# Load order, row statistics on two engines, and the last output tile of a fused attention and gMLP kernel

## The chip, the cores and the metric

The kernel runs on one core of one Trainium2 chip. Time is that of the device, in microseconds (us), for one execution; several runs are made and their median is given. A profile is one execution of its own, recorded by the hardware profiler. Engine names in it: PE is TensorE (PEld its weight loads), DVE is VectorE, ACT is ScalarE, POOL is GpSimd, SP is SyncE, which here issues DMAs.

## What is computed

Two blocks share one normalised input, and their outputs are added to the input (S = 2048 tokens, D = 512):

```python
xn = _layernorm(x)                       # no gain, no bias, eps 1e-5
# A: sliding, dilated attention, 32 heads of 16, 8 keys per token at distance 0, 2, .. 14
qkv = xn @ wqkv
logits = (q . k[shifted]) * 16 ** -0.5   # masked where the key lies before the start
a = softmax(logits) . v[shifted]  @ wo
# B: gMLP with a spatial gate
z = gelu(xn @ w_in)                      # 2048 x 1376
z1, z2 = z[:, :688], layernorm(z[:, 688:])
b = (z1 * (w_sp @ z2 + b_sp)) @ w_out    # w_sp is 2048 x 2048
out = x + a + b
```

All inputs and the output are bfloat16.

## The kernel before

Tokens are cut into 16 tiles of 128. The order of work is written out by hand: each engine runs its instructions in program order, and semaphores for the true dependencies are set by the framework.

**Loads.** All loads are issued by SP, in the order of lines 165 to 180: x tile 0 (128 KB), x tiles 1 to 3, `w_z2` (the half of `w_in` that gives z2) in two column halves of 344, then `wqk` in four parts between x blocks 1 and 2 (four tiles each), `wv`, the gate's bias, and x block 3. The x blocks use three buffers, so block 3 waits for block 0.

**Normalising the input.** For each token tile VectorE computes mean and variance (`ln_stats`, L187 and L188). Tiles 0 to 3 get their inverse root from ScalarE's Sqrt (`roots`, L196) and a reciprocal on VectorE; tiles 4 to 15 get it from two Newton steps of three operations each, behind three seed operations on integers, all on VectorE (`ln_newton`, L202 to L208), for four tiles at a time. `ln_apply` (L192) writes the normalised tile. It is transposed into `xnT` by TensorE for tiles 0 to 3 (`transpose_pe`, L213, with a copy on ScalarE for tiles 0 and 1, L215, and on VectorE for tiles 2 and 3, L217), and by a DMA issued by SP for the others (`transpose_dma`, L220).

**The opening.** `spin` issues matmuls on ones that nobody reads. Tile 0 is normalised, transposed and multiplied by `w_z2` (`z2_start`, L226, 8 matmuls of 344 columns: two column halves by four chunks of the contraction); then tile 1; then tiles 2 and 3 are normalised and transposed. All statistics of tiles 4 to 15 stand next in VectorE's order. TensorE goes on with `qk_chunk` (L258: for 512 tokens and 128 channels of q and of k, 8 matmuls of 512 columns), with z2 tiles 2 and 3 between the chunks, then z2 tiles 4 to 6 and the chunks of the next 512 tokens, and so on. ScalarE empties each result: Gelu for z2 (L232), a square for its statistics (L236), copies for q and k (L261). Three pairs of PSUM banks go round (`bank_pair`).

**The middle.** VectorE multiplies q by shifted k (`products`, L287), TensorE sums them over each head's channels (`reduce_heads`, L296), and softmax follows; v comes from `v_pair` (L271). For each output tile j the spatial mix (`mix`, L463, 32 matmuls) and z1 (`z1_tile`, L475) give the gated product, which a DMA transposes into `uT` (L486). VectorE meanwhile forms the attention output `op` (`av_ops`, L529 to L538), in portions that `vector_work` hands out.

**The end.** `op` holds 14 of each head's 16 channels for direct use; the other two are copied by `op_rest` (L518, eight DMAs for each half of the tokens) into free rows of the last chunk of `uT`. The output tiles are formed in two passes (`pair`, L587) over two groups of four tiles: 112 matmuls of `op` by `wo_r` (L597), then for each tile six of `uT` by `wout` (L605). VectorE adds x (L609) and SP writes the tile out (L610).

Of the kernel before, what the change touches and what calls it, by code (L numbers as in the profile page):

```python
# [45 lines left out]
def kernel(  # L46
# [38 lines left out]
    def bank_pair(name, two=False):  # L85
        turn[0] += 1
        pool = ps_b if turn[0] % 3 == 0 and not two else ps_a
        return pool.tile([P, 2, 512], F32, name=name, tag="mm")
# [71 lines left out]
    def load_x(b):  # L160
        t = xqp.tile([P, 4, D], BF16, name="xq")
        SP.dma_start(t[:], x2[b * 4 * P:(b + 1) * 4 * P, :].rearrange("(i p) d -> p i d", p=P))
        xq.append(t)

    x0 = xqp.tile([P, 4, D], BF16, name="xq")
    SP.dma_start(x0[:, 0, :], x2[0:P, :])
    SP.dma_start(x0[:, 1:4, :], x2[P:4 * P, :].rearrange("(i p) d -> p i d", p=P))  # L167
    xq.append(x0)
    for hh in range(2):
        fsl = slice(hh * FHALF, (hh + 1) * FHALF)  # L170
        SP.dma_start(w_z2[:, :, fsl], w_in_r[:, :, FH + hh * FHALF:FH + (hh + 1) * FHALF])  # L171
    wqk_s = wqkv_r[:, :, 0:2 * D].rearrange("p k (s n) -> p k s n", s=2)
    for ch in range(2):
        csl = slice(ch * D // 2, (ch + 1) * D // 2)
        for s in range(2):
            SP.dma_start(wqk[:, :, s, csl], wqk_s[:, :, s, csl])
        load_x(1 + ch)
    SP.dma_start(wv[:], wqkv_r[:, :, 2 * D:3 * D])
    SP.dma_start(b16[:], B_b_sp.rearrange("(j p) -> j p", p=P))
    load_x(3)  # L180
# [4 lines left out]
    def ln_stats(i):  # L185
        xs = xq[i // 4][:, i % 4, :]
        V.bn_stats(stats[:, i, :], xs)  # L187
        V.bn_aggr(mv[:, i, :], stats[:, i, :])  # L188
# [9 lines left out]
    def ln_newton(a, b):  # L198

        sl = slice(a, b)  # L200
        y, h, t = rstd[:, sl], hv[:, sl], nt[:, sl]
        V.tensor_scalar(h, mv[:, sl, 1], EPS, -0.5 / NEWTON_K, ALU.add, ALU.mult)  # L202
        V.tensor_scalar(t.bitcast(I32), h.bitcast(I32), 1, 0x3FFFFFFF, ALU.logical_shift_right, ALU.bitwise_and)
        V.tensor_scalar(y.bitcast(I32), t.bitcast(I32), -1, SEED, ALU.mult, ALU.add)
        for c in NEWTON_C:
            V.tensor_tensor(t, y, y, ALU.mult)
            V.tensor_tensor(t, t, h, ALU.mult)
            V.scalar_tensor_tensor(y, t, c, y, ALU.add, ALU.mult)  # L208

    def transpose_pe(i, xn):  # L210
        pt = ps_aux.tile([P, C, P], BF16, name="pt", tag="aux")
# [9 lines left out]

    def z2_start(i):
        pz = bank_pair("pzb")
        for hh in range(2):
            for kc in range(C):
                PE.matmul(pz[:, hh, 0:FHALF], xnT[:, kc, i * P:(i + 1) * P],  # L226
                          w_z2[:, kc, hh * FHALF:(hh + 1) * FHALF],
                          start=(kc == 0), stop=(kc == C - 1))
        return pz

    def z2_gelu(i, pz):
        A.activation(z2[:, i, :].rearrange("p (a b) -> p a b", a=2), pz[:, :, 0:FHALF],  # L232
# [5 lines left out]
    def z2_tile(i):  # L238
        z2_gelu(i, z2_start(i))
# [13 lines left out]
    def qk_chunk(b, c):  # L253
        tsl = slice(b * 512, (b + 1) * 512)
        pq = bank_pair("pq")
        for s in range(2):
            for kc in range(C):
                PE.matmul(pq[:, s, :], wqk[:, kc, s, c * P:(c + 1) * P], xnT[:, kc, tsl],  # L258
                          start=(kc == 0), stop=(kc == C - 1))
        at = HALO + b % 2 * 512  # L260
        A.copy(qk[b // 2][:, :, c, at:at + 512], pq[:])  # L261

    wv_v = wv[:].rearrange("p k (h d) -> p k d h", d=DH)
    xnT_g = xnT[:].rearrange("p c (b k t) -> p c b k t", b=NB, k=NG)
# [65 lines left out]
        wsps[j] = t  # L330


    ln_stats(0)
    roots(0, 1)
    V.reciprocal(rstd[:, 0:1], rstd[:, 0:1])
    transpose_pe(0, ln_apply(0))
    spin(4)
    pz0 = z2_start(0)
    ln_stats(1)
    roots(1, 2)  # L340
    ln_stats(2)
    V.reciprocal(rstd[:, 1:2], rstd[:, 1:2])
    transpose_pe(1, ln_apply(1))
    spin(4)
    pz1 = z2_start(1)
    ln_stats(3)
    roots(2, 4)
    z2_gelu(0, pz0)
    z2_gelu(1, pz1)
    V.reciprocal(rstd[:, 2:4], rstd[:, 2:4])  # L350
    xn2 = ln_apply(2)
    xn3 = ln_apply(3)
    transpose_pe(2, xn2)
    transpose_pe(3, xn3)
    spin(3)


    for b in range(4, NT, 4):
        for i in range(b, b + 4):
            ln_stats(i)  # L360
        ln_newton(b, b + 4)
        for i in range(b, b + 4):
            transpose_dma(i, ln_apply(i))


    qk_chunk(0, 0)
    qk_chunk(0, 1)
    z2_tile(2)
    z2_square(0)
    qk_chunk(0, 2)  # L370
    z2_tile(3)
    qk_chunk(0, 3)
    z2_square(1)
    pb = ps_aux.tile([P, NT], BF16, name="pb", tag="aux")
    PE.transpose(pb[:], b16[:], ident[0:NT, 0:NT])
    A.copy(b_col[:], pb[:])
# [134 lines left out]
    wout = late2.tile([P, MCH, D], BF16, name="wout")  # L511
    G.memset(wout[32:64, MCH - 1, :], 0.0)

    def op_rest(hb):

        for k in range(NG):
            for e in range(2):
                SP.dma_start(uT[64 + 32 * e:96 + 32 * e, MCH - 1, hb * SB + k * TG:hb * SB + (k + 1) * TG],  # L518
                             op[32 * k:32 * k + 32, DHA + e, hb * TG:(hb + 1) * TG])

    def av_ops():
        for hb in range(NB):
            for q in range(2):
                osl = slice(hb * TG + q * P, hb * TG + (q + 1) * P)
                pws = []
                for p in range(4):
                    off = HALO - DIL * (W - 1 - 2 * p) + q * P
                    pw = pwp.tile([P, 2, DH, P], BF16, name="pw")
                    V.tensor_tensor(pw[:], shifted(vp[:, :, hb, off:off + P]),  # L529
                                    a_sb[:, 2 * p:2 * p + 2, osl].unsqueeze(2).broadcast_to([P, 2, DH, P]), ALU.mult)  # L530
                    yield 2.3
                    pws.append(pw)
                    if p % 2 == 1:
                        V.tensor_tensor(pws[p - 1][:], pws[p - 1][:], pw[:], ALU.add)  # L534
                        yield 2.3
                V.tensor_tensor(pws[0][:], pws[0][:], pws[2][:], ALU.add)
                yield 2.3
                V.tensor_tensor(op[:, :, osl], pws[0][:, 0], pws[0][:, 1], ALU.add)  # L538
                yield 1.2
            if hb == 0:  # L540
                softmax_norm(1, smp)
                yield 5.5
# [19 lines left out]
    for j in range(3, NT):  # L562
        z1_tile(j, mix(j))
        if j == 3:
            pair_b.close()
            ps_o = [ctx.enter_context(tc.tile_pool(name="ps_o0", bufs=4, space=PSUM, reuse_waits="tile"))]
        vector_work(4.6)
        gate_out(j - 1)
        if j == 5:
            SP.dma_start(wout[:, 0:MCH - 1, :], B_w_out[0:(MCH - 1) * P, :].rearrange("(m p) n -> p m n", p=P))  # L570
            SP.dma_start(wout[0:FTAIL, MCH - 1, :], B_w_out[(MCH - 1) * P:FH, :])
            for e in range(2):
                SP.dma_start(wout[64 + 32 * e:96 + 32 * e, MCH - 1, :],
                             A_wo.rearrange("(h d) n -> d h n", d=DH)[DHA + e])
        if 6 <= j < 10:
            k = j - 6
            SP.dma_start(wo_r[32 * k:32 * k + 32, :, :], A_wo.rearrange("(h d) n -> h d n", d=DH)[:, 0:DHA, :])
        if 11 <= j < 13:
            load_xr(j - 11)
        if j == 13:  # L580
            op_rest(0)
    gate_out(NT - 1)
    pair_a.close()


    ps_o.append(ctx.enter_context(tc.tile_pool(name="ps_o1", bufs=4, space=PSUM, side="right", reuse_waits="tile")))
    for pair in range(2):  # L587
        if pair:
            vector_work(1e9)
            op_rest(1)  # L590
        pos = {}
        for jj in (2 * pair, 2 * pair + 1):
            for k in range(NG):
                pos[jj, k] = ps_o[jj % 2].tile([P, D], F32, name="po")
            for d in range(DHA):
                for k in range(NG):
                    PE.matmul(pos[jj, k][:], op[32 * k:32 * k + 32, d, jj * P:(jj + 1) * P],  # L597
                              wo_r[32 * k:32 * k + 32, d, :],
                              start=(d == 0), stop=False, tile_position=(32 * k, 0))
        for jj in (2 * pair, 2 * pair + 1):  # L600
            hb, q = jj // 2, jj % 2
            for k in range(NG):
                i = 8 * hb + 2 * k + q
                for m in range(MCH):
                    PE.matmul(pos[jj, k][:], uT[:, m, i * P:(i + 1) * P], wout[:, m, :],  # L605
                              start=False, stop=(m == MCH - 1))
                vector_work(2.0)
                ot = otp.tile([P, D], BF16, name="ot")
                V.tensor_tensor(ot[:], pos[jj, k][:], xrs[jj][:, k, :], ALU.add)  # L609
                SP.dma_start(out2[i * P:(i + 1) * P, :], ot[:])  # L610
            if jj + 2 < 4:
                load_xr(jj + 2)

# [29 lines left out]
```

## Time and profile before

| | |
|---|---|
| median of 3 runs | 210.63 us (210.3 to 211.45) |
| the profiled execution | 211.15 us |
| its span, first to last instruction | 208.8 us |
| PE busy, share of the span | 201.8 us, 97% |
| DVE busy | 166.8 us, 80% |
| ACT busy | 93.1 us, 45% |
| POOL busy | 6.0 us, 3% |
| granted TensorE clock | 1.0 of full speed |

The page cuts the span into 40 slices of 5.2 us. TensorE's row reads 7 in the first slice and 3 in the last, and 9 (90% or more busy) in nearly all between. VectorE is at 4 to 9 in the first nine slices. GpSimd does its few operations in the first 4 us (masks and a unit matrix) and clears small pads later.

Two costs stand beside the matmuls of the opening: the 16 statistics of L187 take 670 ns each, and the 16 applications of L192 take 409 ns each. The median load of `w_z2` lands 5.0 us after its issue, that of an x block 6.6 us after, an output tile 1.7 us after.

### The profile page before, as it was taken

The page shows a single profiled execution, that of the slowest core. Times are in us where ns is not written, and L with a number is a line of the kernel's source. Part 1 is how long each engine was busy: PE and PEld are TensorE (multiplying, and loading weights), DVE is VectorE, ACT ScalarE, POOL GpSimd, SP SyncE. Part 2 cuts the span into 40 slices and gives each one's busy share as a digit, 9 for nine tenths or more (in the row PEclk, how much of TensorE's full clock was granted, in tenths as well). Part 3 has the DMA queues.
Part 4 walks back from the last instruction along what each step waited for, and adds up shares of the span by engine and source line. Part 5 has one row for each costly group of instructions (what it writes and reads, how often), then busy time and mean ns, then how long its engine had stood idle before and what let it go on. Part 6 is the DMA issues. An engine that isn't in the chain of part 4 may idle for free.

```text
span 208.8 us, 3966 instructions
## 1 busy us (share of the span) xinstructions
PE 201.8 (97%) x1638; PEld 118.0 (57%) x1645; DVE 166.8 (80%) x198; ACT 93.1 (45%) x144; POOL 6.0 (3%) x34
## 2 busy tenths in 40 slices
PE   7799999999999999999999999999999999999993
PEld 4445544454556665556666666666666664444441
DVE  4689986986187699999999999999999965582252
ACT  3468888766788998326733121233333221000000
POOL 5000000000000000000000000000000000000000
PEclk9999999999999999999999999999999999999999
DMA  6993335999000003442965999999654232038332
GB/s 168 312 331 82 76 75 102 171 262 205 5 0 3 3 0 22 104 100 52 150 149 128 228 163 223 199 189 193 145 148 108 56 72 48 25 78 255 92 107 78
DMA packets 68817, 25.62 MB, mean 123 GB/s; under 512 B 57168, under 2 KB 68672, under 8 KB 68672
## 3 DMA queue, kind: packets, MB, share of 16 engines
q1 hardware_dynamic: 68800, 25.38, 56.6%
q8 instruction: 13, 0.21, 0.4%
q14 instruction: 4, 0.03, 0.0%
HBM read 9.79 MB, written 2.10 MB: 57 GB/s over the span
## 4 chain that ended last, share of the span: by engine, by line
PE 94%; DMA 3%; DVE 1%; SPq 1%; issue 1%; ACT 0%
PE pg L463 36%; PE pq L258 13%; PE po L605 10%; PE pz L475 9%; PE pzb L226 9%; PE pv L271 7%; PE po L597 6%; PE pl L296 4%; DMA w_z<-in_B_w_in_dram 3%; DVE xnT L217 0%; DVE ot L609 0%; ACT xnT L215 0%; SPq L171 0%; PE pt L213 0%; SPq L167 0%
## 5 line engine op out<-in xcount | busy, mean ns | idle before, releaser
L463 PE MATMUL pg<-z,wspT 128*128 128x344 bf16 x512 | 77.3, 309 | 0.0
L463 PEld LDWEIGHTS <-wspT 128*128 128x128 bf16 x512 | 49.9, 98 | 25.2 <-issue 0.8
L287 DVE TENSOR_TENSOR pr<-qk 128x8192 bf16<-128x8192 bf16 x8 | 35.1, 4421 | 6.5 <-PE pl L296 6.5
L466 ACT ACTIVATE gs<-pg,b_col 128x688 bf16<-128x688 f32 x16 | 13.4, 835 | 54.0 <-PE pg L463 54.0
L529 DVE TENSOR_TENSOR pw<-vp,a_sb 128x4096 bf16<-128x4096 bf16 x16 | 36.1, 2283 | 0.0
L258 PE MATMUL pq<-xnT,wqk 128*128 128x512 bf16 x123 | 28.9, 379 | 0.7 <-DVE xnT L217 0.4
L609 DVE TENSOR_TENSOR ot<-po,xr 128x512 bf16<-128x512 f32 x16 | 10.9, 688 | 16.4 <-PE po L605 16.3
L226 PE MATMUL pzb<-w_z,xnT 128*128 128x344 bf16 x128 | 20.7, 309 | 1.5 <-DMA w_z<-in_B_w_in_dram 1.0
L475 PE MATMUL pz<-w_z,xnT 128*128 128x344 bf16 x128 | 21.3, 309 | 0.0
L605 PE MATMUL po<-wout,uT 128*128 128x512 bf16 x94 | 20.6, 379 | 0.3 <-issue 0.3
L258 PEld LDWEIGHTS <-wqk 128*128 128x128 bf16 x128 | 12.3, 98 | 15.0 <-issue 1.4
L261 ACT CAST qk<-pq 128x1024 bf16<-128x1024 f32 x16 | 16.2, 1012 | 8.4 <-PE pq L258 8.2
L534 DVE TENSOR_TENSOR pw<-pw 128x4096 bf16<-128x4096 bf16 x8 | 18.3, 2287 | 0.1
L226 PEld LDWEIGHTS <-xnT 128*128 128x128 bf16 x128 | 12.1, 98 | 9.5 <-issue 2.0
L475 PEld LDWEIGHTS <-xnT 128*128 128x128 bf16 x128 | 12.4, 98 | 6.8 <-issue 0.8
L605 PEld LDWEIGHTS <-uT 128*128 128x128 bf16 x96 | 9.2, 98 | 11.7 <-issue 0.8
L271 PE MATMUL pv<-xnT,wv 128*32 128x512 bf16 x256 | 14.9, 380 | 0.0
L480 ACT ACTIVATE z<-pz 128x688 bf16<-128x688 f32 x16 | 11.9, 744 | 5.6 <-PE pz L475 4.8
L236 ACT ACTIVATE junk<-z 128x688 bf16<-128x688 bf16 x16 | 12.5, 780 | 0.1
L597 PE MATMUL po<-wo_r,op 32*128 32x512 bf16 x224 | 12.4, 374 | 0.0
L232 ACT ACTIVATE z<-pzb 128x688 bf16<-128x688 f32 x16 | 11.8, 740 | 0.6 <-PE pzb L226 0.6
L187 DVE BATCH_NORM_STATS2 stats<-xq 128x6 f32<-128x512 bf16 x16 | 10.7, 670 | 1.7 <-DMA xq<-in_A_x_dram 1.7
(73 smaller groups left out, 139.2 us busy)
## 6 DMA issues: line engine op xcount, KB each, us to landing
xr<-in_A_x_dram SPq DMA_DIRECT2D x4, 512.0 KB, 4.8
out_dram<-ot SPq DMA_DIRECT2D x16, 128.0 KB, 1.7
wo_r<-in_A_wo_dram SPq DMA_DIRECT2D x4, 448.0 KB, 4.9
xq<-in_A_x_dram SPq DMA_DIRECT2D x3, 512.0 KB, 6.6
wqk<-in_A_wqkv_dram SPq DMA_DIRECT2D x4, 256.0 KB, 6.2
w_z<-in_B_w_in_dram SPq DMA_DIRECT2D x2, 344.0 KB, 5.0
w_z<-in_B_w_in_dram SPq DMA_DIRECT2D x1, 688.0 KB, 6.6
wout<-in_B_w_out_dram SPq DMA_DIRECT2D x1, 640.0 KB, 5.0
```

What stands on the lines that cost most here:

```text
L226: PE.matmul(pz[:, hh, 0:FHALF], xnT[:, kc, i * P:(i + 1) * P], w_z2[:, kc, hh * FHALF:(hh + 1) * FHALF], start=(kc == 0), stop=(kc == C - 1))
L258: PE.matmul(pq[:, s, :], wqk[:, kc, s, c * P:(c + 1) * P], xnT[:, kc, tsl], start=(kc == 0), stop=(kc == C - 1))
L261: A.copy(qk[b // 2][:, :, c, at:at + 512], pq[:])
L271: PE.matmul(pv[32 * k:32 * k + 32, dd, :].rearrange("p (b t) -> p b t", b=NB), wv_v[:, kc, 2 * d2 + dd, :], xnT_g[:, kc, :, k, :], start=( ...
L287: V.tensor_tensor(pr[:], qk[hb][:, 0, :, HALO:HALO + SB].unsqueeze(1).broadcast_to([P, 2, C, SB]), shifted(qk[hb][:, 1, :, off:off + SB]), ...
L463: PE.matmul(pg[:, hh, 0:FHALF], wsps[j][:, k, :], z2[:, k, hh * FHALF:(hh + 1) * FHALF], start=(k == 0), stop=(k == NT - 1))
L466: A.activation(gs[:], pg[:, :, 0:FHALF], ACT.Identity, bias=b_col[:, j:j + 1])
L475: PE.matmul(pz[:, hh, 0:FHALF], xnT[:, kc, j * P:(j + 1) * P], w_z1[:, kc, hh * FHALF:(hh + 1) * FHALF], start=(kc == 0), stop=(kc == C - 1))
L529: V.tensor_tensor(pw[:], shifted(vp[:, :, hb, off:off + P]), a_sb[:, 2 * p:2 * p + 2, osl].unsqueeze(2).broadcast_to([P, 2, DH, P]), ALU.mult)
L534: V.tensor_tensor(pws[p - 1][:], pws[p - 1][:], pw[:], ALU.add)
L597: PE.matmul(pos[jj, k][:], op[32 * k:32 * k + 32, d, jj * P:(jj + 1) * P], wo_r[32 * k:32 * k + 32, d, :], start=(d == 0), stop=False, til ...
L605: PE.matmul(pos[jj, k][:], uT[:, m, i * P:(i + 1) * P], wout[:, m, :], start=False, stop=(m == MCH - 1))
```

## The change

There are three edits.

1. *The opening.* The loads are issued in another order: x tiles 0 and 1 singly, the first two contraction chunks of `w_z2` (full rows of 688 columns), x tiles 2 and 3, the other two chunks, x block 1, `wqk` in two parts (q, then k), x block 2, and so on. Tiles 0 to 3 are normalised with one root each. z2 tiles 0 and 1 run their first two chunks ahead of the other two, and z2 tiles 2 and 3 run ahead of any q or k. A chunk of q and k becomes `qk_pair` for the first 512 tokens: two chunks of q, or of k, in one bank pair. There are fewer `spin` matmuls.
2. *The roots of tiles 4 to 15* are formed for two tiles at a time. The seeds stay on VectorE; each Newton step is four operations on GpSimd, and a pair's tiles are normalised after the statistics and seeds of the next pair.
3. *The end.* The second `op_rest` moves ahead of the second group's matmuls of the first pass and is issued by ScalarE's queue. The last output tile is formed in two column halves of 256, in new PSUM banks; its attention part and x are added ahead of time into `rest`.

```diff
     SP.dma_start(x0[:, 0, :], x2[0:P, :])
-    SP.dma_start(x0[:, 1:4, :], x2[P:4 * P, :].rearrange("(i p) d -> p i d", p=P))
+    SP.dma_start(x0[:, 1, :], x2[P:2 * P, :])
+    SP.dma_start(w_z2[:, 0:2, :], w_in_r[:, 0:2, FH:F])
+    SP.dma_start(x0[:, 2:4, :], x2[2 * P:4 * P, :].rearrange("(i p) d -> p i d", p=P))
+    SP.dma_start(w_z2[:, 2:4, :], w_in_r[:, 2:4, FH:F])
     xq.append(x0)
-    for hh in range(2):
-        fsl = slice(hh * FHALF, (hh + 1) * FHALF)
-        SP.dma_start(w_z2[:, :, fsl], w_in_r[:, :, FH + hh * FHALF:FH + (hh + 1) * FHALF])
-    wqk_s = wqkv_r[:, :, 0:2 * D].rearrange("p k (s n) -> p k s n", s=2)
-    for ch in range(2):
-        csl = slice(ch * D // 2, (ch + 1) * D // 2)
-        for s in range(2):
-            SP.dma_start(wqk[:, :, s, csl], wqk_s[:, :, s, csl])
-        load_x(1 + ch)
+    load_x(1)
+    for s in range(2):
+        SP.dma_start(wqk[:, :, s, :], wqkv_r[:, :, s * D:(s + 1) * D])
+    load_x(2)
...
         for c in NEWTON_C:
-            V.tensor_tensor(t, y, y, ALU.mult)
-            V.tensor_tensor(t, t, h, ALU.mult)
-            V.scalar_tensor_tensor(y, t, c, y, ALU.add, ALU.mult)
+            G.tensor_tensor(t, y, y, ALU.mult)
+            G.tensor_tensor(t, t, h, ALU.mult)
+            G.tensor_scalar(t, t, c, None, ALU.add)
+            G.tensor_tensor(y, y, t, ALU.mult)
...
+    def z2_part(i, pz, kc):
         for hh in range(2):
-            for kc in range(C):
-                PE.matmul(pz[:, hh, 0:FHALF], xnT[:, kc, i * P:(i + 1) * P],
+            PE.matmul(pz[:, hh, 0:FHALF], xnT[:, kc, i * P:(i + 1) * P],
...
+    def qk_pair(b, s, c2):
+        tsl = slice(b * 512, (b + 1) * 512)
+        pq = bank_pair("pq")
+        for cc in range(2):
+            c = 2 * c2 + cc
+            for kc in range(C):
+                PE.matmul(pq[:, cc, :], wqk[:, kc, s, c * P:(c + 1) * P], xnT[:, kc, tsl],
+                          start=(kc == 0), stop=(kc == C - 1))
+        at = HALO + b % 2 * 512
+        A.copy(qk[b // 2][:, s, 2 * c2:2 * c2 + 2, at:at + 512], pq[:])
...
+    def recip(i):
+        V.reciprocal(rstd[:, i:i + 1], rstd[:, i:i + 1])
     ln_stats(0)
     roots(0, 1)
-    V.reciprocal(rstd[:, 0:1], rstd[:, 0:1])
-    transpose_pe(0, ln_apply(0))
-    spin(4)
-    pz0 = z2_start(0)
     ln_stats(1)
     roots(1, 2)
+    recip(0)
+    transpose_pe(0, ln_apply(0))
+    recip(1)
+    spin(2)
+    transpose_pe(1, ln_apply(1))
+    spin(2)
+    pz0 = bank_pair("pzb")
+    pz1 = bank_pair("pzb")
+    for i, pz in ((0, pz0), (1, pz1)):
+        for kc in range(2):
+            z2_part(i, pz, kc)
     ln_stats(2)
...
+    roots(2, 3)
     ln_stats(3)
-    roots(2, 4)
+    roots(3, 4)
+    for kc in range(2, C):
+        z2_part(0, pz0, kc)
     z2_gelu(0, pz0)
-    z2_gelu(1, pz1)
-    V.reciprocal(rstd[:, 2:4], rstd[:, 2:4])
+    recip(2)
     xn2 = ln_apply(2)
+    recip(3)
     xn3 = ln_apply(3)
     transpose_pe(2, xn2)
+    for kc in range(2, C):
+        z2_part(1, pz1, kc)
     transpose_pe(3, xn3)
-    spin(3)
-    for b in range(4, NT, 4):
-        for i in range(b, b + 4):
-            ln_stats(i)
-        ln_newton(b, b + 4)
-        for i in range(b, b + 4):
-            transpose_dma(i, ln_apply(i))
-    qk_chunk(0, 0)
-    qk_chunk(0, 1)
+    z2_gelu(1, pz1)
     z2_tile(2)
+    z2_tile(3)
+    groups = tuple((i, i + 2) for i in range(4, NT, 2))
+    prev = None
+    for g in groups + (None,):
+        if g:
+            for i in range(*g):
+                ln_stats(i)
+            ln_newton(*g)
+        if prev:
+            for i in range(*prev):
+                transpose_dma(i, ln_apply(i))
+        prev = g
+    qk_pair(0, 0, 0)
     z2_square(0)
-    qk_chunk(0, 2)
-    z2_tile(3)
-    qk_chunk(0, 3)
+    qk_pair(0, 0, 1)
     z2_square(1)
+    qk_pair(0, 1, 0)
+    qk_pair(0, 1, 1)
...
+    def last_tile(i, rest):
+        ot = otp.tile([P, D], BF16, name="ot")
+        for h in range(2):
+            ns = slice(h * D // 2, (h + 1) * D // 2)
+            po = ps_o[0].tile([P, D], F32, name="po")
+            for m in range(MCH):
+                PE.matmul(po[:, ns], uT[:, m, i * P:(i + 1) * P], wout[:, m, ns],
+                          start=(m == 0), stop=(m == MCH - 1))
+            V.tensor_tensor(ot[:, ns], po[:, ns], rest[:, ns], ALU.add)
+            SP.dma_start(out2[i * P:(i + 1) * P, ns], ot[:, ns])
     for pair in range(2):
-        if pair:
-            vector_work(1e9)
-            op_rest(1)
...
+                if (jj, k) == (3, NG - 1):
+                    last_tile(i, rest)
+                    continue
...
+                if (jj, k) == (2, 0):
+                    rest = pwp.tile([P, D], F32, name="rest", tag="pw")
+                    V.tensor_tensor(rest[:], pos[3, NG - 1][:], xrs[3][:, NG - 1, :], ALU.add)
+            if jj == 0:
+                vector_work(1e9)
+                op_rest(1, A)
```

More of the change, by code (lines that the diff above doesn't have):

```diff
@@ L223, in z2_start @@
         pz = bank_pair("pzb")
+        for kc in range(C):
+            z2_part(i, pz, kc)
+        return pz
+    def z2_part(i, pz, kc):
         for hh in range(2):
-            for kc in range(C):
[L226 to L229, printed above, removed]
+            PE.matmul(pz[:, hh, 0:FHALF], xnT[:, kc, i * P:(i + 1) * P],
+                      w_z2[:, kc, hh * FHALF:(hh + 1) * FHALF],
+                      start=(kc == 0), stop=(kc == C - 1))
     def z2_gelu(i, pz):
@@ L261, in qk_chunk @@
         A.copy(qk[b // 2][:, :, c, at:at + 512], pq[:])
+    def qk_pair(b, s, c2):
[3 more added lines that the diff above has]
+            c = 2 * c2 + cc
+            for kc in range(C):
+                PE.matmul(pq[:, cc, :], wqk[:, kc, s, c * P:(c + 1) * P], xnT[:, kc, tsl],
+                          start=(kc == 0), stop=(kc == C - 1))
+        at = HALO + b % 2 * 512
+        A.copy(qk[b // 2][:, s, 2 * c2:2 * c2 + 2, at:at + 512], pq[:])
     wv_v = wv[:].rearrange("p k (h d) -> p k d h", d=DH)
@@ L330, in load_wsp @@
         wsps[j] = t
+    def recip(i):
+        V.reciprocal(rstd[:, i:i + 1], rstd[:, i:i + 1])
     ln_stats(0)
     roots(0, 1)
-    V.reciprocal(rstd[:, 0:1], rstd[:, 0:1])
-    transpose_pe(0, ln_apply(0))
-    spin(4)
-    pz0 = z2_start(0)
     ln_stats(1)
     roots(1, 2)
+    recip(0)
[8 more added lines that the diff above has]
+        for kc in range(2):
+            z2_part(i, pz, kc)
     ln_stats(2)
[L342 to L345, printed above, removed]
+    roots(2, 3)
     ln_stats(3)
-    roots(2, 4)
+    roots(3, 4)
+    for kc in range(2, C):
+        z2_part(0, pz0, kc)
     z2_gelu(0, pz0)
-    z2_gelu(1, pz1)
-    V.reciprocal(rstd[:, 2:4], rstd[:, 2:4])
+    recip(2)
     xn2 = ln_apply(2)
+    recip(3)
     xn3 = ln_apply(3)
     transpose_pe(2, xn2)
+    for kc in range(2, C):
+        z2_part(1, pz1, kc)
     transpose_pe(3, xn3)
-    spin(3)
-    for b in range(4, NT, 4):
-        for i in range(b, b + 4):
-            ln_stats(i)
-        ln_newton(b, b + 4)
-        for i in range(b, b + 4):
-            transpose_dma(i, ln_apply(i))
-    qk_chunk(0, 0)
-    qk_chunk(0, 1)
-    z2_tile(2)
+    z2_gelu(1, pz1)
+    z2_tile(2)
+    z2_tile(3)
[11 more added lines that the diff above has]
+    qk_pair(0, 0, 0)
     z2_square(0)
-    qk_chunk(0, 2)
-    z2_tile(3)
-    qk_chunk(0, 3)
+    qk_pair(0, 0, 1)
     z2_square(1)
+    qk_pair(0, 1, 0)
+    qk_pair(0, 1, 1)
     pb = ps_aux.tile([P, NT], BF16, name="pb", tag="aux")
@@ L512, with op_rest @@
     G.memset(wout[32:64, MCH - 1, :], 0.0)
-    def op_rest(hb):
+    def op_rest(hb, q):
         for k in range(NG):
             for e in range(2):
-                SP.dma_start(uT[64 + 32 * e:96 + 32 * e, MCH - 1, hb * SB + k * TG:hb * SB + (k + 1) * TG],
+                q.dma_start(uT[64 + 32 * e:96 + 32 * e, MCH - 1, hb * SB + k * TG:hb * SB + (k + 1) * TG],
                              op[32 * k:32 * k + 32, DHA + e, hb * TG:(hb + 1) * TG])
@@ L527, in av_ops @@
                     off = HALO - DIL * (W - 1 - 2 * p) + q * P
-                    pw = pwp.tile([P, 2, DH, P], BF16, name="pw")
+                    pw = pwp.tile([P, 2, DH, P], BF16, name="pw", tag="pw")
                     V.tensor_tensor(pw[:], shifted(vp[:, :, hb, off:off + P]),
@@ L580 @@
         if j == 13:
-            op_rest(0)
+            op_rest(0, SP)
     gate_out(NT - 1)
     pair_a.close()
+    def last_tile(i, rest):
[8 more added lines that the diff above has]
+            SP.dma_start(out2[i * P:(i + 1) * P, ns], ot[:, ns])
     ps_o.append(ctx.enter_context(tc.tile_pool(name="ps_o1", bufs=4, space=PSUM, side="right", reuse_waits="tile")))
     for pair in range(2):
-        if pair:
-            vector_work(1e9)
-            op_rest(1)
         pos = {}
@@ L598 @@
                               wo_r[32 * k:32 * k + 32, d, :],
-                              start=(d == 0), stop=False, tile_position=(32 * k, 0))
+                              start=(d == 0), stop=((jj, k, d) == (3, NG - 1, DHA - 1)), tile_position=(32 * k, 0))
         for jj in (2 * pair, 2 * pair + 1):
```

## The prediction

> **What bounds the kernel now.** I read the shares of the chain that ended last, then that chain in order of time, then the timelines of its first 40 and last 45 us. Line 4 of the page gives the chain by engine:
>
> ```profile
> PE 94%; DMA 3%; DVE 1%; SPq 1%; issue 1%; ACT 0%
> ```
>
> The same chain in order of time (start, duration, what) shows where it leaves TensorE:
>
> ```profile
> 2.26 5.62 DMA w_z<-in_B_w_in_dram
> ...
> 7.92 0.74 PE pzb L226 x4
> ...
> 9.57 1.34 PE pzb L226 x8
> ...
> 12.07 0.38 PE pq L258
> ...
> 205.52 0.02 issue
> 205.54 0.69 DVE ot L609
> ```
>
> From 12.07 to 205.52 us the pieces are matmuls end to end. So time can be won only ahead of 12.07, where TensorE has done just two z2 tiles (16 matmuls of L226), and behind 205.52; in between, an engine ahead of TensorE can only add a wait. Matmul work is unchanged, so every us TensorE gets ahead stays won unless a later operand is late.
>
> **The front, step by step.** Of 128 KB and more per load, bytes ahead of a load set its landing. Summing the 1-us stretches of the DMA rate: 0.54 MB by 4.0 us, 0.82 by 5.0, 1.05 by 6.0, 1.36 by 7.0, 2.04 by 9.0, 2.7 by 11.0. Against this the second half of w_z2 (1.23 MB with what is ahead) landed at 7.88, 1.3 us behind the sum, and x1 (3.90 + 7.3 us to landing = 11.2, 2.28 MB) 1.4 behind; the first x0 loads were 0.3 to 0.7 behind. With the new order I get: x0 tile 1 (0.26 MB) 3.7; w_z2 chunks 0 and 1 (0.61) 5.1; x0 tiles 2 and 3 (0.88) 6.1; w_z2 chunks 2 and 3 (1.23) 7.9; x1 (1.75) 9.5; the q half of wqk (2.28) 11.2; its k half 12.9. SP issues 12 loads instead of 13.
>
> The operations are priced from these rows of the timeline (start, duration, engine, line):
>
> ```profile
> 3.07 0.69 DVE L187 BATCH_NORM_STATS2 stats<-xq 128x6 f32<-128x512 bf16 x1 [1.69 <-DMA xq<-in_A_x_dram]
> 3.79 0.18 DVE L188 BATCH_NORM_AGGREGATE mv<-stats 128x2 f32<-128x6 f32 x1
> 4.01 0.29 ACT L196 ACTIVATE rstd<-mv,eps_t 128x1 f32<-128x1 f32 x1 [1.93 <-DVE mv L188]
> 4.54 0.41 DVE L192 TENSOR_SCALAR xn<-xq,mv,rstd 128x512 bf16<-128x512 bf16 x1
> 5.50 0.59 ACT L215 COPY xnT<-pt 128x512 bf16<-128x512 bf16 x1 [1.20 <-PE pt L213]
> 9.72 1.28 ACT L232 ACT_TABLE_LOAD   x1
> ```
>
> Statistics of tile 1 now stand ahead of the reciprocal of tile 0: 3.87 to 4.76. Apply 0 runs 4.86 to 5.27 (4.54 to 4.95 before, 0.3 later), its transposes 5.32, the copy on ScalarE 5.8, operand ready 6.46. Tile 1: apply to 5.8, operand 6.97. The first halves of z2 tiles 0 and 1 (4 matmuls, 0.59 us each at the chain's 1.17 us per tile) fill 6.46 to 7.64, while w_z2 chunks 2 and 3 are in flight: that is the reordering's point, since before all eight matmuls of tile 1 stood behind 7.88. Then 7.9 to 8.5 ends tile 0. Statistics of tiles 2 and 3: 6.1 to 7.7; apply 2 to 8.2; apply 3, behind its own Sqrt and reciprocal, to 8.7. Transposes 2 at 8.5, tile 1's rest 8.75 to 9.35, transposes 3 to 9.6, copies of tiles 2 and 3 ready at 9.5 and 10.3. z2 tiles 2 and 3: 9.6 to 11.95 (2 x 1.17). The Gelu table load (8.05 to 9.35) and gelu 0 (to 10.1) free tile 3's bank in time. First qk matmul: 11.95, its weights there since 11.2. Before, it started at 12.07 with z2 tiles 2 and 3 still to do: won 2 x 1.17 + 0.12 = **2.45**. I take 2.3, for the 0.05 to 0.14 us of issue that the chain shows at each change of producer; bounds 1.3 (w_z2's rest a further us late, as it follows smaller loads) to 2.9 (landing at 7.4, as rows are 1376 B and not 688 B, and then apply 2 limits).
>
> **Roots on GpSimd.** Removed from VectorE are 3 x 6 operations, 0.2 us apart; three more groups add 3 x 3 seed operations at 0.2: -3.6 + 1.8 = -1.8 us of VectorE time. What decides is GpSimd's chain, eight dependent operations for two columns. The trace has no arithmetic on GpSimd; nearest are dependent pairs there:
>
> ```profile
> 1.58 0.21 POOL L108 TENSOR_SCALAR_AFFINE_SELECT rsel<-rsel 128x32 bf16<-128x32 bf16 x1
> 1.86 0.21 POOL L110 TENSOR_SCALAR_AFFINE_SELECT rsel<-rsel 128x32 bf16<-128x32 bf16 x1
> 3.60 0.33 POOL L114 TENSOR_SCALAR_AFFINE_SELECT mask<-mask 32x128 f32<-32x128 f32 x1
> ```
>
> 0.28 us from start to start, 0.07 of it between end and start. Low end: the 0.10 us of a one-column memset (L627) + 0.07 = 0.17, chain 1.4. High end: the 0.516 us of wout's memset (L512) + 0.07 = 0.59, chain 4.7. I take 0.28, since an affine select reads and writes as the new ones do: 2.2, with 0.1 of handing over 2.3. Cover on VectorE from one pair's seeds to its apply: apply of the pair before (0.41 + 0.33), two statistics at 0.79, seeds 0.6, together **2.9**; for the first pair, which has no apply in front, 2.2. So it is hidden up to 0.35 us an operation.
>
> Behind an apply that waits on VectorE stand the next statistics, then products(0, 0); behind them the transposes on SP and TensorE. Due times: statistics of tile 4 start at 10.3 (x1 landed 9.5), seeds end 12.6, apply 4 at 15.0; transposes issue 1.3 us apart and land 2.5 after, so tile 7 (issue 19.75) lands at 22.3; due at qk_chunk(1, 0), 25.02 - 2.3 = 22.7. Last apply ends 12.6 + 5 x 3.0 (with a handover) + 2.3 + 0.75 = 30.65.
>
> ```profile
> 33.27 13.09 DVE L287 TENSOR_TENSOR pr<-qk 128x8192 bf16<-128x8192 bf16 x3
> ...
> 38.37 1.05 PE L296 MATMUL pl<-pr,rsel 128*32 128x512 bf16 x16
> ```
>
> The first product (4.42) must end for L296, now at 38.37 - 2.3 = 36.1; so VectorE must be free of statistics by 31.5. Slack 0.85, where it was 2.5 (31.1 against 33.6). Cost taken: 0; bounds 0 and (12.6 + 6 x 4.8 + 0.75) - 31.5 = 10.7 us.
>
> A rule that speaks against this: the Trainium skill, "SBUF — State Buffer", section "Who interferes with whom", has VectorE and GpSimd share one port pair under an exclusive lock, which tensor_scalar in a two-port mode takes. No overlap of the two shows in this trace. By it the two applies of a pair would hold up GpSimd by at most their 0.74 us (L192), an estimated chain of 3.0 instead of 2.3, and 0.7 lost of the slack of 0.85: still no loss. The statistics have one input and by that section do not contend.
>
> **The end.** The last add covers 256 columns instead of 512: L609 takes 0.688 for 512 PSUM columns, and L215's neighbour row L321 0.294 for 256; scaled from L609 with 0.16 fixed, 0.42. Won 0.27 (bounds 0.2 to 0.4). The first half's add and its DMA (issue 0.4 us) lie beside the second half's matmuls (0.64 us); were they not hidden, they would cost 0.4. The final transfer is 64 KB in as many rows: 0 to 0.2, taken 0. Twelve 256-column matmuls instead of six of 512: 0.05 more, at the 98 ns weight loads hidden under 107 ns; at L475's 0.146 us pitch it would be 0.47. `rest` adds 0.69 us to VectorE at 197, where it idles 0.60 in each 1.29: worn off in two tiles. The remaining AV work ended at 184.4 already, ahead of the point it is now forced at, so vector_work(1e9) is empty. op_rest(1), 8 issues, leaves SP for ScalarE's queue, idle since 173; TensorE ran L605 at 195.20 without waiting for it: 0.
>
> Sum: 2.3 + 0.27 - 0.05 = **2.5 us**. The profiled execution took 211.15 (span 208.8), 0.5 over the median of 210.63; the difference is carried to the median: **208.1**. A measurement of this kernel can't tell less than about 0.5% (1.05 us) from no change.
>
> **Rivals.**
> 1. *GpSimd's chain outgrows its cover* (slower). Place: apply(prev) on VectorE. At 0.45 us an operation the chain is 3.7, the last apply ends at 12.6 + 6 x 3.7 + 0.75 = 35.55, TensorE waits 4.05 at L296: 210.63 - 2.5 + 4.05 = 212.2. It decides from 0.41 us an operation, where the loss eats the 2.5. For it: the memset of 0.516 and no row of arithmetic; against: 0.28 for reads and writes of 32 elements, where the new ones have 2. The skill's "GPSIMD Engine Reference", "Instruction dispatch", gives some 6 us for the first call of a freshly loaded kernel; no row here shows it, and by it the first pair would be 6 us late and the estimate about 212. 15%.
> 2. *The loads, not the order, hold the front.* x1 or wqk (0.7 us of margin each) or w_z2 land 1 to 1.5 later; gain 1.0 to 1.5: 209.4. For it: the lag of 0.3 to 1.4 us behind the sum; against: bytes ahead of w_z2's end are the same. 12%.
> 3. *Given back later*: the front is won, but tiles 6 and 7 (slack 0.4) or the products (0.85) come 2 us late through port waits: 210.3, no change. 6%.
>
> Forecast 67%, own range 207.2 to 209.3: 2.9 + 0.4 + 0.1 won, to 1.3 won. To leave no more than two in ten outside I go up to 210.6, rival 3's side and the mild part of rival 1. Faster by over 0.5% (below 209.6): 67 + 8 of rival 2 = 75; within: 11; slower: 14.
>
> **What would show it.** First L258-like matmul near 11.9 with four z2 tiles behind it; no TensorE wait on `pr` at the first L296; GpSimd starts 0.28 apart and VectorE waiting at L192 at most on the first pair; last add near 0.42. A VectorE wait at L192 in each pair would make the prediction wrong.

## The result, and the profile after

The changed kernel takes 208.28 us (median of 4 runs, 207.78 to 208.4) against 210.48 beside it: a ratio of 0.9873, 95% interval 0.9829 to 0.9917 (the two medians alone give 0.9895, inside the interval). Two more sets of runs of the same kernel gave 207.98 (ratio 0.9874, 0.9855 to 0.9894) and 208.14 (0.9886, 0.9867 to 0.9904). The forecast was 208.1, faster. The profiled execution took 208.18, its span 206.5 (before: 211.15 and 208.8).

An execution takes longer than its span from first to last instruction: by 2.28 to 2.49 us in the runs of the kernel before, by 1.67 to 1.79 in those of the changed kernel. So some 0.6 us of the gain lies outside the span, where no view shows it. In the medians of the spans the gain is 1.8 and 2.1 us in the two sessions that have them for both kernels. The two parts of the change tested alone below each move this remainder a little (2.01 to 2.14 without the new end, 2.19 to 2.28 with the new end alone); what it consists of is not known.

The shares of the chain that ended last, in the changed kernel:

```profile
PE 91%; DVE 3%; DMA 3%; POOL 1%; issue 1%
```

GpSimd is new there, and the same chain in order of time (start, duration, what) shows where it enters and where TensorE lost something again:

```profile
2.97 0.71 DVE stats L185
...
6.77 1.80 PE pzb L229 x12
...
12.37 0.20 POOL nt L204
...
14.59 0.74 DVE xn L190 x2
...
16.41 4.11 DMA xnT<-xn
20.52 0.05 issue
20.56 2.51 PE pzb L229 x16
...
202.10 1.32 PE po L622 x12
203.42 0.02 issue
203.44 0.42 DVE ot L624
```

The load of `w_z2` that filled the chain from 2.26 to 7.88 before is not on it in this profile: the chain now runs through the statistics of the first tiles, and TensorE multiplies from 6.77. Later it leaves TensorE once more, at a transpose by DMA that landed 4.11 us after 16.41, and TensorE's next z2 matmul began at 20.56.

TensorE's rows in the timeline say how much was won and given back. Before, z2 tiles 4 to 6 stand here:

```profile
21.51 3.67 PE L226 MATMUL pzb<-w_z,xnT 128*128 128x344 bf16 x24
```

and in the changed kernel:

```profile
11.77 7.07 PE L272 MATMUL pq<-xnT,wqk 128*128 128x512 bf16 x32
18.91 1.34 PE L229 MATMUL pzb<-w_z,xnT 128*128 128x344 bf16 x8
20.56 2.51 PE L229 MATMUL pzb<-w_z,xnT 128*128 128x344 bf16 x16 [0.31 <-DMA xnT<-xn]
36.26 1.05 PE L310 MATMUL pl<-pr,rsel 128*32 128x512 bf16 x16
```

The first q and k matmul starts at 11.77 with four z2 tiles behind it; before, at 12.07 with two: 12.07 + 2 x 1.17 - 11.77 = 2.64 us ahead. z2 tile 4 starts at 18.91, before at 21.51: 2.60. The head sums of L310 start at 36.26, before at 38.37: 2.11. So 0.49 us was given back between tiles 4 and 7. From there on the distance stays: the matmuls end at 203.42 instead of 205.52 (2.10), and the last add takes 0.42 instead of 0.69. Together 2.37, and the spans differ by 2.3.

### The profile page after: what moved, and what is told of

Read it like the earlier page. It is cut to its first block, busy times and chain, and to the rows that moved or that the text cites. A ratio compares the mean times of both kernels' runs of the same rounds, so it can differ in the third digit from the quotient of the medians.

```text
span 206.5 us, 4016 instructions
## 1 busy us (share of the span) xinstructions
PE 201.7 (98%) x1644; PEld 118.3 (57%) x1644; DVE 166.2 (81%) x192; ACT 93.6 (45%) x145; POOL 16.1 (8%) x82
## 4 chain that ended last, share of the span: by engine, by line
PE 91%; DVE 3%; DMA 3%; POOL 1%; issue 1%
PE pg L493 36%; PE pq L260 10%; PE po L647 10%; PE pz L505 9%; PE pzb L229 8%; PE pv L285 7%; PE po L636 6%; PE pl L310 4%; DMA xnT<-xn 2%; DVE stats L185 2%; DMA xq<-in_A_x_dram 1%; PE pt L212 1%; PE po L622 1%; DVE xn L190 1%; DVE mv L186 0%
## 5 line engine op out<-in xcount | busy, mean ns | idle before, releaser
L651 DVE TENSOR_TENSOR ot<-po,xr 128x512 bf16<-128x512 f32 x15 | 10.2, 689 | 15.2 <-PE po L647 15.1
L260 PE MATMUL pq<-xnT,wqk 128*128 128x512 bf16 x96 | 21.7, 379 | 0.0
L647 PE MATMUL po<-wout,uT 128*128 128x512 bf16 x90 | 19.8, 379 | 0.0
L260 PEld LDWEIGHTS <-wqk 128*128 128x128 bf16 x96 | 9.2, 98 | 11.1 <-issue 0.8
L647 PEld LDWEIGHTS <-uT 128*128 128x128 bf16 x90 | 8.7, 98 | 11.0 <-issue 0.8
L263 ACT CAST qk<-pq 128x1024 bf16<-128x1024 f32 x12 | 12.1, 1012 | 5.8 <-PE pq L260 5.8
```

## The experiments

The two parts of the change that can matter alone are the opening with the load order, and the end; the pairs on GpSimd only have to stay hidden. That was the theory (A) against rivals that give GpSimd, the freed SP queue or plain chance a share. All times are medians, with the ratio to the kernel before in the same session.

| run | us | ratio, 95% interval |
|---|---|---|
| fours on VectorE | 208.43 | 0.9874, 0.9852 to 0.9896 |
| pairs on VectorE | 211.25 | 1.0002, 0.9979 to 1.0024 |
| opening without the end | 208.8 | 0.9894, 0.9870 to 0.9919 |
| end without the opening | 210.26 | 0.9994, 0.9970 to 1.0018 |
| wv late | 207.28 | 0.9823, 0.9800 to 0.9847 |
| wv late, again | 207.63 | 0.9856, 0.9837 to 0.9874 |
| fours on VectorE, wv late | 208.07 | 0.9884, 0.9860 to 0.9908 |
| four more operations on GpSimd | 210.29 | 0.9965, 0.9938 to 0.9991 |
| eight more | 219.8 | 1.0439, 1.0418 to 1.0460 |
| before, again | 211.44 | 1.0045, 1.0013 to 1.0077 |

The last row is the kernel before against itself, and bounds what a difference here can mean: its own two sets of runs differ by 0.45%. Where less than that is at stake, the profiles decide below, not the times.

**Roots in fours on VectorE, the rest of the change kept.**

```diff
-            G.tensor_tensor(t, y, y, ALU.mult)
-            G.tensor_tensor(t, t, h, ALU.mult)
-            G.tensor_scalar(t, t, c, None, ALU.add)
-            G.tensor_tensor(y, y, t, ALU.mult)
+            V.tensor_tensor(t, y, y, ALU.mult)
+            V.tensor_tensor(t, t, h, ALU.mult)
+            V.scalar_tensor_tensor(y, t, c, y, ALU.add, ALU.mult)
...
+    for b in range(4, NT, 4):
+        for i in range(b, b + 4):
+            ln_stats(i)
+        ln_newton(b, b + 4)
+        for i in range(b, b + 4):
+            transpose_dma(i, ln_apply(i))
```

> The changed kernel, but with the roots of tiles 4 to 15 in groups of four on VectorE, as before the change. Theory A (the new opening and the last tile carry the whole gain, GpSimd's part only has to stay hidden): statistics start at 9.98 us, the last apply ends near 9.98 + 19.3 = 29.3, ahead of the 31.06 at which products(0, 0) starts; tile 4 is ready some 0.5 later, tile 7 at the same time: 208.3 +- 0.4, the first L296-like matmul after products near 36.3. Rival B (relief of VectorE is part of the gain): slower than the changed kernel by 0.6 or more, 208.9 or above.

Measured 208.43, ratio 0.9874: the same as the changed kernel. TensorE waits for the transpose of tile 5 here too, and the head sums start at 36.36. The opening of this profile was 0.3 later (first q and k matmul at 12.08); from that matmul to the head sums it takes 24.28 us, the changed kernel 24.32 to 24.49 in its three profiles. Theory A holds in the kernel as changed: GpSimd's part of the change adds nothing that can be measured.

**Pairs kept, Newton steps on VectorE.** The diff is the first half of the one above.

> The changed kernel with the Newton steps on VectorE again (six operations instead of eight on GpSimd), pairs and their order kept. Theory A: a pair then costs VectorE 1.6 + 0.6 + 1.2 + 0.74 = 4.1 us instead of 2.9, the last apply ends near 34.8 instead of 29.3, products are 3 us late, and TensorE waits about 3 us in all: 211.3 (210.3 to 212). Rival B' (products have more slack than that): below 209.3.

Measured 211.25. The chain that ended last in this run shows the road: VectorE's last applications at 32.5, a product, then TensorE.

```profile
32.52 1.38 DVE xn L190 x4
33.90 0.09 DVE qk L423
33.99 4.34 DVE pr L300
38.33 0.04 issue
38.37 1.05 PE pl L309 x16
```

The last application ends at 33.90 (34.8 expected), and the head sums start at 38.37 instead of 36.26. So smaller groups cost VectorE three sets of seeds and Newton steps more, and take the whole gain of the opening; moving the steps to GpSimd returns it. Pairs and GpSimd have to be judged together, and together they come to nothing in the kernel as changed.

**The opening without the end, and the end without the opening.**

```diff
-    def op_rest(hb, q):
+    def op_rest(hb):
...
-    def last_tile(i, rest):
...
+        if pair:
+            vector_work(1e9)
+            op_rest(1)
```

> The changed kernel with the end of before: last tile whole, second op_rest on SP between the passes. Theory A: TensorE ends at the same time as in the changed kernel (203.4 us), and the last add is 0.69 instead of 0.42: slower than the changed kernel by 0.25 to 0.35, 208.55. Rival C (freeing SP of op_rest before the last tiles matters too): slower by 0.6 or more.

> The kernel before with only the new end (last tile in two halves, attention part and x added ahead, second op_rest earlier on ScalarE's queue). Theory A: TensorE ends 0.05 later at most, the last add is 0.42 instead of 0.69: faster than before by 0.2 to 0.3, ratio 0.9987. Rival C (the freed SP queue or the earlier op_rest is worth more): 0.6 or more faster, ratio 0.997 or less.

Measured 208.8 (0.9894) and 210.26 (0.9994). The times alone don't separate 0.27 us from nothing. The profiles do: with the old end the chain closes like this,

```profile
192.94 10.32 PE po L635 x47
203.27 0.02 issue
203.29 0.69 DVE ot L639
```

and with the new end alone like this:

```profile
194.27 9.01 PE po L617 x41
203.28 1.32 PE po L592 x12
204.61 0.02 issue
204.63 0.42 DVE ot L594
```

From the first matmul of the last group to the last 10.33 and 10.34 us: twelve narrow matmuls cost nothing. The add is 0.27 shorter. From the first q and k matmul to the last matmul it is 193.45 us in the kernel before and 193.47 with the new end alone, so the freed SP queue and the earlier copies of `op_rest` give TensorE nothing.

**wv loaded behind the transposes of tiles 4 to 7.**

```diff
-    SP.dma_start(wv[:], wqkv_r[:, :, 2 * D:3 * D])
     SP.dma_start(b16[:], B_b_sp.rearrange("(j p) -> j p", p=P))
...
                 transpose_dma(i, ln_apply(i))
+            if prev[0] == 6:
+                SP.dma_start(wv[:], wqkv_r[:, :, 2 * D:3 * D])
```

> The changed kernel with the load of wv (512 KB, first used at 37 us) behind the transposes of tiles 4 to 7 in SP's order. In the changed kernel TensorE waits 0.5 us for tile 5, whose transpose landed 4.1 us after its issue where 2.5 is usual. Theory D (transposes of tiles 4 and 5 stand behind the tail of the x and wv loads on the same queue): the loads end 1.5 us sooner, both land in 2.5 to 3, the wait is gone: faster than the changed kernel by 0.4 to 0.5, 207.8. Rival E (the transposes are slow for another reason, such as two in a row or a start after other transfers): they still take 3.8 and 4.1, no gain.

> The changed kernel with wv loaded behind the transposes of tiles 4 to 7, once more, now on the same chip as the changed kernel. Theory D: 0.5 to 0.8 us faster than the changed kernel, ratio to before 0.9845 or less. Rival (the gain of the first run was the chip's): within 0.2 of the changed kernel.

> The changed kernel itself, as the measure for the run beside it: ratio to before 0.987 to 0.988.

> The changed kernel itself, on the same chip as the three runs beside it, as their measure: 208.3 +- 0.3 by every theory; TensorE waits near 20 us for the transpose of tile 5.

Measured 207.28 and, beside the changed kernel at 208.14, 207.63: 0.5 us faster in the same session. That is less than the bound above, so the profiles have to say it: from the first q and k matmul to the head sums the two with wv late take 23.97 and 24.03 us, the changed kernel's three 24.32 to 24.49. The two changed-kernel runs came out at 0.9874 and 0.9886. What the DMA view gives for the transposes of tiles 4 and 5 (issues, then us to landing), in the changed kernel and then with wv late:

```profile
xnT<-xn SPq DMA_TRANSPOSE x1, 3.8
...
xnT<-xn SPq DMA_TRANSPOSE x2, 4.0
```

```profile
xnT<-xn SPq DMA_TRANSPOSE x1, 2.5
xnT<-xn SPq DMA_TRANSPOSE x1, 2.4
```

In the changed kernel the loads still moved 234 GB/s in the stretch from 15 to 16 us, where the first transpose was issued (15.03); with wv late they moved 46 from 14 to 15 and 0 from 15 to 16. The last of the loads queued there, x block 3, landed at 18.0 (issued at 9.63, 8.4 to landing); with wv late it landed at 14.8 (8.52 and 6.3). TensorE then runs z2 tiles 4, 5 and 6 in one piece:

```profile
18.61 3.67 PE L228 MATMUL pzb<-w_z,xnT 128*128 128x344 bf16 x24
```

The slow landings moved with the load: in this run the transposes of tiles 8 and 9, issued next after wv, took 4.2 and 3.5, and the first matmuls that read those start at 30.2 us. In the second run the transposes of tiles 4 and 5 took 2.8 and 3.3, and TensorE still ran the three tiles in one piece. So theory D is shown as far as that the loads ahead of these transposes made TensorE wait; how the loads slow a transpose is not. By the medians this version is the fastest of those measured.

**Fours on VectorE with wv late.** The edits of the first experiment and of the one just above, together.

> Groups of four with the roots on VectorE (no GpSimd) and wv loaded behind the transposes of tiles 4 to 7. Theory A (GpSimd's part is not needed): in the run with fours apply 4 began 0.8 us later than in the changed kernel, the transposes start 1.35 apart and with an idle queue land after 2.5, so tiles 4 to 7 land near 18.3, 19.7, 21.0 and 22.4 against 18.7, 19.9, 21.0 and 22.3 needed: 207.4, within 0.3 of the run with pairs on GpSimd and wv late. Rival B (the earlier start of the pairs shows once the queue is free): 207.9 or more.

Measured 208.07, ratio 0.9884 beside the changed kernel's 0.9874: rival B's number, but not by its road. Tile 5's transpose took 3.4 instead of 2.5, with no load in front of it, and TensorE waited for it:

```profile
17.10 3.41 DMA xnT<-xn
20.52 0.05 issue
20.56 2.51 PE pzb L227 x16
```

z2 tile 4 starts at 19.06 in this profile, so tile 5 was due 1.17 later, at 20.23: a wait of 0.33. In the kernel before and in the run with fours the second of the first four took 3.4 too; in the pairs with wv late it took 2.4 in one run and 3.3 in the other. Why the second is slow stays open. The rest of the lateness lies ahead of all this: the first q and k matmul starts at 11.95, with wv late at 11.50 and 11.44, though the kernels are alike up to there. From that matmul to the head sums this run takes 24.30 us, against 23.97 and 24.03 with pairs. So once the loads are out of the way, pairs on GpSimd are worth some 0.3 us over fours on VectorE in these profiles, by when the transposes start and land, not by VectorE's load.

**A longer chain on GpSimd.** Two, then four, more operations in each Newton step:

```diff
             G.tensor_scalar(t, t, c, None, ALU.add)
+            for _ in range(2):
+                G.tensor_scalar(t, t, 1.0, None, ALU.mult)
```

> The changed kernel with two more operations in each Newton step on GpSimd (a product with 1.0), twelve operations a pair instead of eight: the chain grows from 2.2 to some 3.4 us, past the cover of 2.9 on VectorE. Theory F (slack as worked out: VectorE must be free of statistics by 31.8): last apply ends at 12.3 + 6 x 3.45 + 0.75 = 33.75, TensorE waits 2 us at the first head sums: 210.3 (209.7 to 211). Rival G (GpSimd's chain is off the path altogether, or the products have more slack): below 209.

> As the run with four more, with four more in each Newton step, sixteen operations a pair: chain 4.6 us. Theory F: last apply at 12.3 + 6 x 4.65 + 0.75 = 41, TensorE waits some 9 us for transposes and products: 217.5 (216 to 219). Rival G: below 210.

Measured 210.29 and 219.8. With four more the chain of waits ends the statistics at 33.7 (33.75 expected), and the head sums start at 38.18, 1.9 later than in the changed kernel:

```profile
33.71 0.09 DVE qk L426
33.80 4.34 DVE pr L303
...
38.18 1.05 PE pl L312 x16
```

The slack as worked out is shown. With eight more, the last application ends at 41.26 (41 expected) and the head sums start 9.5 late; the other 2.3 us over the expectation fit what the clock cost (2.6, below).

**The kernel before once more.**

> The kernel before, profiled once more. In its first profile TensorE's first q and k matmul starts at 12.07 us, 0.5 us of the time above the median; in the run with the new end alone, which has the same opening, it starts at 11.14 and TensorE does not wait for w_z2 at all. Theory H (the landing of w_z2 differs between executions by up to a microsecond, so the first profile shows the front too late): first q and k matmul between 11.1 and 11.9, time 209.9 to 210.8. Rival (something of the end moved the opening): 12.0 to 12.1 again.

12.21 and 211.28: the expectation missed, and this run alone would speak for the rival. But the opening of the run with only the new end is instruction for instruction that of the kernel before, and there TensorE ran all of tile 0 without waiting for `w_z2`:

```profile
6.22 1.52 PE L226 MATMUL pzb<-w_z,xnT 128*128 128x344 bf16 x8
...
11.14 2.10 PE L258 MATMUL pq<-xnT,wqk 128*128 128x512 bf16 x8 [0.39 <-DVE xnT L217]
```

What sets the landing of `w_z2`, near 7.9 to 8.0 in two profiles and at 7.0 in a third, isn't settled; the third is the fastest of its kernel's twelve runs (209.79 against a median of 210.26). Against the early opening the gain of the new one is 11.14 + 2.34 - 11.77 = 1.7 and not 2.64 us. The new opening varies too: its first q and k matmul starts between 11.36 and 12.08 in the eleven profiles that have it.

## Why the prediction was right, by its steps

- *The front*, taken at 2.3 within 1.3 to 2.9: 2.64 in the two profiles, with the landing of `w_z2` as the uncertain part, as said; against an early landing it is 1.7, in the lower part of the range. The first operand and the halves of z2 came within about 0.3 of the times worked out (6.77 for 6.46, first q and k matmul 11.77 for 11.95). `w_z2` was not waited for in the changed kernel's first profile, but the chain still runs through its second half in two of the eleven profiles of the new opening (the third of the changed kernel and the one with four more operations), where it landed at 7.7; 7.9 had been worked out. In another (fours on VectorE) x tiles 2 and 3 held it up, landing at 6.4 where 6.1 had been worked out. No run separates the order of the loads from the halves of z2 and from the order of TensorE's work, so what each of these gives is open.
- *GpSimd's chain*, 0.28 us an operation, 2.2 for eight: 12.37 to 14.56 in the first pair, 2.19. An affine select was the right row for tiny arithmetic. VectorE waits at the applications only once, for the last pair, which has no statistics behind it:

```profile
28.60 0.73 DVE L190 TENSOR_SCALAR xn<-xq,mv,rstd 128x512 bf16<-128x512 bf16 x2 [1.79 <-POOL rstd L207]
```

  The forecast had allowed such a wait on the first pair only. It costs nothing: VectorE is done at 29.3 and then idles until 31.06, when ScalarE's copy of q and k is ready for the products. The last application ended at 29.3 where 30.65 was expected: the pairs came every 2.87 us instead of 3.0, and the statistics began at 9.98 instead of 10.3. In the first pair GpSimd was done as VectorE came to it, at 14.59. The rival that the chain outgrows its cover was decided where it had been put: with 0.285 us an operation twelve operations do it, eight don't.
- *The step that was mis-sized*: "transposes issue 1.3 us apart and land 2.5 after". Tiles 4 and 5 landed after 3.8 and 4.1, when the new opening issues them behind loads that had not all landed; with wv out of the way the wait is gone; the sum had looked at tile 7 (expected at 22.3, due 22.7) and not at tile 5. That cost 0.49 us in the first profile, and it is the third rival's place (transposes late) by another mechanism than its port waits.
- *The end*: 0.27 for the add, as worked out; the 0.05 for the narrow matmuls was not there.
- *The sum*, 2.5 against 2.2, 2.8 and 2.4 in the medians of three sessions. That it fits is in part luck. Its terms all lie inside the span: in the two profiles the opening, less the wait for tile 5, and the add make 2.37 there, but the first profile of the kernel before shows a late `w_z2`, and in the medians of the spans it is 1.8 and 2.1. The 0.6 us outside the span, for which the forecast had no term, fills the gap.
- *The shared port*. The Trainium skill, "SBUF — State Buffer", "Who interferes with whom", would have let the two applications hold up GpSimd for up to 0.74 us a pair. The timeline of the changed kernel shows the overlap (VectorE's applications of a pair at 17.46 to 18.19):

```profile
17.63 0.29 POOL L204 TENSOR_TENSOR nt<-rstd 128x2 f32<-128x2 f32 x1 [0.83 <-DVE rstd L202]
18.00 0.25 POOL L205 TENSOR_TENSOR nt<-nt,hv 128x2 f32<-128x2 f32 x1
...
18.90 0.19 POOL L204 TENSOR_TENSOR nt<-rstd 128x2 f32<-128x2 f32 x1
19.17 0.19 POOL L205 TENSOR_TENSOR nt<-nt,hv 128x2 f32<-128x2 f32 x1
```

  The first two operations take 0.29 and 0.25 instead of 0.19 each, and start to start 0.37 and 0.33 instead of 0.27 and 0.28: 0.15 us a pair, with VectorE's two at 0.73 as before. It is so in four of the five pairs whose chain meets applications; in the second pair of the kernel it is 0.06. So the overlap costs GpSimd a fifth of the bound at most; that the port is what does it is not shown. Of the code loading that the Trainium skill, "GPSIMD Engine Reference", "Instruction dispatch", gives some 6 us for, nothing shows: the first operation began 0.07 us after the last seed and took 0.19.

## What to carry to other kernels

Where one engine's work fills the span, count how far it is ahead at the first operation that repeats in both kernels, then follow that distance along the timeline: each place where it shrinks is a wait with a name, and mending the one found here (a load not needed for 20 us, in front of transposes needed in 4) was worth about a fifth of the whole change. A step moved earlier can run into other traffic, so its latency need not be that of the old place. Look also at what the time holds beyond the span of the instructions: here a quarter of the gain was there, and no row of a profile explains it. Work moved to a slower engine is free as long as its chain is shorter than what the first engine does meanwhile, and that border can be worked out and then tested by lengthening the chain.

## What the runs showed of the hardware

With eight more operations on GpSimd, TensorE stood idle from 41.5 to 45.7. In the table by stages (stretch, its length, busy time of TensorE, weight loads, VectorE, ScalarE and GpSimd, granted clock, DMA share, GB/s) the clock fell during the wait:

```profile
43.00:44.00 1.00, 0.00 (x0) 0.00 (x0) 1.00 (x1) 0.00 (x0) 0.00 (x0) 1.00 0.54 109
44.00:45.00 1.00, 0.00 (x0) 0.00 (x0) 1.00 (x1) 0.00 (x0) 0.19 (x2) 0.76 0.16 33
45.00:46.00 1.00, 0.27 (x4) 0.14 (x7) 1.00 (x2) 0.00 (x0) 0.08 (x1) 0.50 1.04 240
...
51.00:52.00 1.00, 1.00 (x8) 0.39 (x5) 1.00 (x1) 0.91 (x1) 0.00 (x0) 0.83 0.62 162
```

It stayed at 0.50 until past 51, and the same head sums and v matmuls took 1.90 and 3.41 us where they take 0.98 and 1.73 in the changed kernel's chain: 2.6 us more, on top of the wait of 4.2. The wait of 1.4 us with four more left the clock at 1.00. The Trainium skill, "TensorE: Matmul & The Clock Gate", Part 1, states a halved clock after at least one idle window of about 3.4 us. The wait of 1.4 agrees; in the longer one the clock fell at 44.5, some 3.0 us after TensorE's last matmul and so a little sooner than a whole window.
